# A gated linear-attention and mixer kernel: the recorded order of its 2,770 operations and their PSUM pools, exchanged from the conversion of w2 on

## The chip, the cores and the metric

The kernel runs on one core of one Trainium2 chip. The metric is the device time of one execution in microseconds (us), taken as the median of several runs. Beside the times there is one profiled execution, whose span (first to last instruction) is what every view of the trace shows.

## The reference

Two blocks follow each other. The first is a gated recurrence per head with a complex decay (4 batches, 8 heads, 768 steps, head dimension 48); the second a token mixer of rank 32 and a channel mixer (384 to 1536 to 384) on its output:

```
a_re_n, a_im_n = a_re * scale, a_im * scale        # scale = min(|a|, 0.999) / (|a| + 1e-6)
for t in range(S):
    S_re, S_im = ar*S_re - ai*S_im + k_t v_t^T, ar*S_im + ai*S_re
    y[:, :, t] = q_t @ S_re
x = y as (4, 768, 384)
u = x + (x^T @ U @ V)^T
out = u + relu(u @ w_ch1) @ w_ch2
```

All is float32.

## The kernel before, in words

**The work.** The 4 x 768 steps are cut into 24 chunks of 128 steps (six for each batch). Two neighbouring chunks form a group (12 of them), and two chunks also form one tile of the mixer (12 tiles, m = 0 to 11).

- For each group `gates` turns a_re and a_im into logarithms of magnitudes and into angles: ACT computes squares, logarithms, exponentials, arctangents and sines (L394), DVE adds and multiplies (L397, L400, L654, L673, L682, L683, L687, L771, L799, L801, L817), PE forms running sums of them (`es ps` and `ef ps` L699, `tot` L751, `ph` L806). Where a phase passes from one chunk to the next, POOL issues a small transfer that adds the last row of `F` onto the first row of the next chunk's angles (L788).
- `prep` multiplies q and k by the gates (L397, writing `qk` and `QKC`) and turns them over on PE (`tr` L873); ACT copies the result out (L884).
- `chain` does one chunk: masked products inside blocks (`inner` L923 and L920, `corners` L984), copied by DVE into `DG` (L935) and by four transfers on SP (L971) into `AT`; state updates `dk` (L1009), and the outputs `y` (L1040, L1048), which ACT copies to `xo`. All these products are small: `inner` L923 has 64 records on PE for 32 products of 32x48 columns.
- `mixer` does one mixer tile: `rank` L1083 and `mixed` L1102 mix tokens, `uTp` L1120 turns the result over, `up` L1135 (m = 0 to 2) or `few` L1235 (m = 3 to 11, with fewer products) goes to 1536 channels, `down` L1326 (m = 0) or L1369 comes back, DVE adds (L400) and the result leaves. For m = 0, `rT` L1149, `rw ps` L1158 and `fix` L1174 bring in the mixed tokens afterwards (DVE L1179).
- The weights come in as raw words in `stage` and are converted by ACT and DVE: for w2 two ACT operations (L394) and three on DVE (L587, L400, L589) for each of six pieces, then three differences of w2 (L617, written back into `stage`). Before m = 3, `combine` forms eight sums of w1 with 13 operations on DVE (L1288).

**The order.** Nothing of the order is left to the compiler. Each operation is handed to a `Plan` with an engine, a cost, the kind it belongs to, and what it reads and writes. `ORDER` holds, for each engine and kind, the place of every operation in one sequence from 0 to 2769; `Plan.order` sorts by these places, asserts that nothing comes before what it needs and that no buffer is taken before its last user, and the operations are issued in that sequence. Each engine and each queue (SP, POOL) takes its own in that order, and one that waits holds up all behind it on the same engine. `BANKS` gives each PSUM tile one of the pools T, A, Y and M (two buffers each). `SPARE` says after which places PE gets filler products of the identity (L1528), in units of 128 columns; a filler goes into a PSUM tile that is free and wide enough at that place.

```
for n in sorted(range(len(at)), key=lambda n: at[n]):
    assert not self.ops[n][5] - done, "an operation comes before what it needs"
...
    buffer(base, "ps" + BANKS[len(wide)], 2, shape, PSUM, padded)
```

The costs that the kernel's text still carries (`c_act`, `c_dve`, `c_dma`) play no part in the issue: the places are constants.

## Time and profile before

| what | us |
|---|---|
| median of 3 runs (lowest, highest) | 621.91 (621.03, 622.38) |
| profiled execution, own time | 619.11 |
| its span | 616.9 |
| PE busy | 598.9 |
| DVE busy | 531.5 |
| ACT busy | 401.8 |

The profiled execution's own time is 2.2 us over its span, and 2.8 us below the median of the runs. A busy PE is one that has a product in flight: products are pipelined, so a short wait between two of them does not show as idle time. PEld is the weight load that belongs to each product. In the views, a row names engine, line, output and input tiles; "issue" as the reason of an idle time means that the engine waited for nothing that the profile shows.

### The profile page before, as it was taken

Reading aid. Unit: us, or ns where it says so; the run is one execution under the profiler, and the core shown is the slowest. Engines: PE = TensorE matmul, PEld = TensorE weight load, DVE = VectorE, ACT = ScalarE, POOL = GpSimd, SP = SyncE. Lnnn points to the kernel's source line nnn. Section 1 sums busy time; section 2 is a strip of 40 time slices with the busy share of each in tenths; the row PEclk is TensorE's granted clock in tenths of the full one; section 3 lists DMA queues with packets and bytes.
Section 4 is the critical chain, followed back from the end, with each engine's and each line's share of the span. In section 5 each row is a group of like instructions: output and inputs, shape, how many; then the busy total and the mean of one; then the engine's idle time right before and its main releaser. Section 6 shows DMA issues by size and latency. Waiting matters only on the chain.

```text
span 616.9 us, 23966 instructions
## 1 busy us (share of the span) xinstructions
PE 598.9 (97%) x10572; PEld 526.8 (85%) x10572; DVE 531.5 (86%) x967; ACT 401.8 (65%) x789; POOL 36.3 (6%) x76
## 2 busy tenths in 40 slices
PE   6998989999999999999999999999999999999998
PEld 3566767656889979899999999899999998999997
DVE  6999999998999999999999999789889986464554
ACT  6999998989888896886696876565652622202020
POOL 4000000000000010000100100000110000000000
PEclk8999999999999999999999999999999999999999
DMA  9865565644233542521523331700122301000000
GB/s 214 198 148 114 136 133 140 157 126 92 50 57 80 92 85 48 109 54 32 113 49 59 86 70 34 137 9 3 39 54 52 65 9 20 21 7 7 20 20 26
DMA packets 173687, 45.77 MB, mean 74 GB/s; under 512 B 167632, under 2 KB 170384, under 8 KB 173584
## 3 DMA queue, kind: packets, MB, share of 16 engines
q1 hardware_dynamic: 171376, 39.90, 31.4%
q0 software_dynamic: 2208, 4.35, 2.1%
q8 instruction: 83, 1.36, 1.0%
q14 instruction: 20, 0.16, 0.1%
HBM read 33.59 MB, written 4.72 MB: 62 GB/s over the span
## 4 chain that ended last, share of the span: by engine, by line
PE 88%; ACT 8%; issue 1%; DVE 1%; DMA 1%; SPq 0%; ACTq 0%
PE down L1369 25%; PE few L1235 20%; PE up L1135 7%; PE dk L1009 4%; PE tr L873 4%; PE y L1048 3%; PE inner L923 3%; PE down L1326 2%; PE inner L920 2%; ACT gate L394 2%; PE y L1040 2%; PE tot L751 2%; PE mixed L1102 2%; PE rank L1083 1%; PE es ps L699 1%; PE up L1528 1%
## 5 line engine op out<-in xcount | busy, mean ns | idle before, releaser
L397 DVE TENSOR_TENSOR QK<-QK,T 96x512 f32<-96x512 f32 (+2 forms) x144 | 102.3, 725 | 1.5 <-PE corners L984 0.9
L1369 PE MATMUL down<-w,h 128*128 128x192 f32 x396 | 72.3, 330 | 0.0
L394 ACT ACTIVATE gate<-gate 128x768 f32<-128x768 f32 (+1 forms) x82 | 64.7, 795 | 9.3 <-DVE GS L801 5.5
L1369 PEld LDWEIGHTS down<-w,h 128*128 128x128 f32 x396 | 64.5, 190 | 1.3 <-issue 0.7
L884 ACT COPY QK<-tr 96x512 f32<-96x512 f32 x96 | 51.0, 587 | 16.9 <-PE tr L873 16.6
L1243 ACT COPY h<-few 128x512 f32<-128x512 f32 x54 | 31.1, 589 | 46.2 <-PE few L1235 34.3
L1135 PE MATMUL up<-uT,w 128*128 128x256 f32 x216 | 50.4, 385 | 0.0
L400 DVE TENSOR_TENSOR xo<-down,xo 128x192 f32<-128x192 f32 (+1 forms) x79 | 30.1, 384 | 23.1 <-PE down L1369 22.7
L1235 PE MATMUL few<-stage,w 128*128 128x128 f32 x360 | 47.1, 277 | 0.0
L1135 PEld LDWEIGHTS up<-uT,w 128*128 128x128 f32 x216 | 39.9, 190 | 5.5
L1235 PEld LDWEIGHTS few<-stage,w 128*128 128x128 f32 x360 | 44.0, 192 | 0.2
L1247 DVE CUSTOM_DVE_ANT_1 h<-few,h 128x512 f32<-128x512 f32 x54 | 35.9, 684 | 8.4 <-PE few L1235 7.0
L397 DVE TENSOR_TENSOR QKC<-qk,cs 128x768 f32<-128x768 f32 x44 | 41.7, 950 | 1.5 <-PE dk L1009 1.1
L989 ACT COPY AT<-corners 32x128 f32<-32x128 f32 x96 | 24.4, 257 | 24.6 <-PE corners L984 23.3
L1235 PE MATMUL few<-stage,sums 128*128 128x128 f32 x288 | 37.8, 278 | 0.0
L1369 PE MATMUL down<-stage 128*128 128x192 f32 x198 | 37.3, 330 | 0.0
L1235 PEld LDWEIGHTS few<-stage,sums 128*128 128x128 f32 x288 | 34.7, 192 | 0.6
L788 POOL DMA_DIRECT2D gate<-F x15 | 12.0, 799 | 362.6 <-DVE w L587 112.5
L1369 PEld LDWEIGHTS down<-stage 128*128 128x128 f32 x198 | 32.2, 190 | 1.0 <-issue 0.6
L873 PEld LDWEIGHTS tr<-ident,QKC 64*96 64x96 f32 x768 | 24.2, 123 | 10.0 <-issue 3.5
L400 DVE TENSOR_TENSOR h<-few,h 128x512 f32<-128x512 f32 x27 | 18.3, 686 | 16.4 <-PE few L1235 12.4
L873 PE MATMUL tr<-ident,QKC 64*96 64x64 f32 x768 | 29.4, 220 | 2.7 <-DVE QKC L397 1.6
(195 smaller groups left out, 1351.2 us busy)
## 6 DMA issues: line engine op xcount, KB each, us to landing
stage<-in_moe_w_ch_dram SPq DMA_DIRECT2D x12, 768.0 KB, 5.0
qk<-in_q_dram SPq DMA_DIRECT2D x24, 192.0 KB, 3.2
qk<-in_k_dram SPq DMA_DIRECT2D x24, 192.0 KB, 3.8
VP<-in_v_dram SPq DMA_DIRECT2D x24, 192.0 KB, 4.1
gate<-in_a_re_dram SPq DMA_DIRECT2D x22, 192.0 KB, 4.1
gate<-in_a_im_dram SPq DMA_DIRECT2D x22, 192.0 KB, 4.1
AT<-DG SPq DMA_DIRECT2D x96, 32.0 KB, 2.0
T<-E SPq DMA_DIRECT2D x48, 48.0 KB, 3.2
```

Of the source, the lines that this page charges most:

```text
L394: return nc.scalar.activation(out=o, in_=i, func=f, **kw)
L397: nc.vector.tensor_tensor(out=o, in0=a, in1=b, op=OP.mult)
L400: nc.vector.tensor_tensor(out=o, in0=a, in1=b, op=OP.add)
L873: nc.tensor.transpose(out=get(*ps[r])[0:DQ, h], in_=get(*qkc)[at, h * DQ:(h + 1) * DQ], identity=ident[at, at], tile_position=(r * HC, 0))
L884: nc.scalar.copy(out=to, in_=a)
L989: ACT(0.36, RR, lambda r=r, u=u: nc.scalar.copy(out=get(*ATi).rearrange("p (a u) t -> p a u t", u=2)[r:r + BLK, :, u, BLK:2 * BLK], in_=ge ...
L1009: nc.tensor.matmul(out=get(*dk[r])[x:x + w, h], lhsT=get(*ks)[at, h * DQ + x:h * DQ + x + w], rhs=get(*VPi)[at, h], start=True, stop=True, ...
L1135: nc.tensor.matmul(out=get(*ps)[:, e], lhsT=w1[:, f, (ff + e) * 128:(ff + e + 1) * 128], rhs=get(*uT)[:, f], start=(f == 0), stop=(f == KD ...
L1235: nc.tensor.matmul(out=get(*ps)[:, q], lhsT=w()[:, q * 128:(q + 1) * 128], rhs=v[0](), start=(n == 0 and q == 0), stop=True, skip_group_ch ...
L1243: ACT(c_act(n3 * CH) - 0.045, RU, lambda i=i, k=k: nc.scalar.copy(out=at(i, k), in_=get(*ps)), [ps], [o])
L1247: DVE(c_dve(n3 * CH), RU, lambda i=i, k=k: nc.vector._custom_dve(dve_ops.TENSOR_ADD_SAT, out=at(i, k), in0=get(*ps), in1=at(i, k), s0=math ...
L1369: nc.tensor.matmul(out=get(*to)[:, part], lhsT=x(j), rhs=y[:, j], start=(first and j == 0), stop=(j == KH - 1), skip_group_check=not first)
```

## The change

The change exchanges the three constants `BANKS`, `ORDER` and `SPARE`. No operation, cost, buffer or function is touched. The first 504 places are the same (up to about 100.5 us of the profiled execution); from there on nearly every place differs: that is the stretch in which the pieces of w2 are converted, m = 0 is finished, and everything behind it. In words it is said of the change that the search for the order charged transfers longer. By kind and engine the same operations are there; 18 units of filler stand behind place 504 before and after.

Cut to the lines on which the text below leans:

```diff
 BANKS = (
-    "...AAAAYYYTTTMMMMMMTTAAYYAATTMMTTTTMMMMMYMMAMAY"
+    "...AAAAYYYMTTAAAATYTYTTMMMMATAYTYATYMTYMMTYYTTATYTYMMYAYT"
...
 ORDER = {
-        ('ACT', 'w2'): {0: [513, 506], 2: [520, 535], 4: [608, 597], 6: [621, 627], 8: [655, 654], 10: [701, 702]},
-        ('DVE', 'w2'): {0: [534, 541, 542], 2: [586, 587, 588], 4: [616, 617, 619], 6: [640, 641, 646], 8: [661, 678, 682], 10: [711, 712, 713], 12:
-        [717, 725, 784]},
+        ('ACT', 'w2'): {0: [513, 507], 2: [575, 543], 4: [588, 602], 6: [630, 649], 8: [652, 655], 10: [707, 706]},
+        ('DVE', 'w2'): {0: [534, 561, 562], 2: [582, 594, 595], 4: [611, 612, 613], 6: [636, 658, 664], 8: [682, 683, 684], 10: [708, 709, 710], 12:
+        [763, 795, 837]},
...
-        ('POOL', 'angles'): {6: [614], 8: [706, 731], 10: [866, 912], 12: [1057], 14: [1265, 1312], 16: [1448, 1521], 18: [1698], 20: [1950, 2023],
+        ('POOL', 'angles'): {6: [616], 8: [700, 756], 10: [874, 934], 12: [1072], 14: [1267, 1292], 16: [1495, 1547], 18: [1731], 20: [1913, 1977],
...
-        ('DVE', 'mixing'): {3: [842, 845, 1024, 1078, 1098, 933, 1062, 1026, 1243, 1250, 1268, 1316, 1280]},
+        ('DVE', 'mixing'): {3: [637, 1027, 988, 1078, 1086, 659, 918, 754, 1098, 1103, 1221, 1247, 1288]},
 }
-SPARE = {20: 8, ... 436: 1, 595: 2, 600: 1, 605: 3, 623: 1, 631: 3, 645: 1, 652: 1, 663: 1, 693: 1, 694: 1, 715: 1, 716: 2}
+SPARE = {20: 8, ... 436: 1, 592: 3, 604: 2, 614: 1, 627: 3, 640: 1, 643: 1, 647: 1, 662: 1, 685: 1, 712: 1, 719: 1, 724: 2}
```

The small products keep their kinds but get other neighbours. Four places of the new sequence on PE, in the order of issue:

```
y L1040 x16, y L1048 x8 x8, inner L923 x32, dk L1009 ...        (chunks 7 and 8)
tr L873 x16, y L1040 x16, y L1048 x8 x8, dk L1009 ...           (chunks 9 and 10)
inner L920 x64, es ps L699, down L1369 ...                      (chunks 10 and 11)
y L1040 x16, y L1048 x8 x8, dk L1009, down L1369 ...            (chunks 13 and 14)
```

Three of the 13 operations of `combine` (places 842, 933 and 1026 before) come at 637, 659 and 754.

## The prediction

> **What bounds the kernel now.** First the page: busy times, the 40 slices, the queue of instruction transfers, and the chain that ended last (shares of it by engine).

> ```profile
> PE 598.9 (97%) x10572; PEld 526.8 (85%) x10572; DVE 531.5 (86%) x967; ACT 401.8 (65%) x789; POOL 36.3 (6%) x76
> ...
> PE   6998989999999999999999999999999999999998
> ...
> DVE  6999999998999999999999999789889986464554
> ...
> PEclk8999999999999999999999999999999999999999
> ...
> q8 instruction: 83, 1.36, 1.0%
> ...
> PE 88%; ACT 8%; issue 1%; DVE 1%; DMA 1%; SPq 0%; ACTq 0%
> ```

> PE carries 88% of the chain and is full from slice 7 on. DVE is full as well up to slice 25, so until about 380 us either can hold up the other; behind that DVE has room. The windows give the same by stage, from 100 us on, where the order begins to differ:

> ```profile
> 100.00:125.00 25.00, 24.91 (x480) 17.94 (x470) 23.34 (x38) 22.21 (x43) 0.96 (x1) 1.00 0.68 161
> 125.00:150.00 25.00, 24.57 (x132) 15.36 (x127) 22.42 (x31) 21.65 (x36) 0.77 (x1) 1.00 0.59 133
> 150.00:175.00 25.00, 24.58 (x403) 20.66 (x401) 23.40 (x37) 21.35 (x38) 1.36 (x2) 1.00 0.18 36
> ...
> 250.00:350.00 100.00, 100.00 (x1929) 93.69 (x1919) 97.15 (x183) 76.41 (x151) 7.99 (x12) 1.00 0.36 70
> 350.00:500.00 150.00, 149.32 (x3055) 141.19 (x3048) 134.32 (x255) 88.48 (x188) 9.34 (x15) 1.00 0.26 52
> ...
> 600.00:617.00 17.00, 13.91 (x86) 13.47 (x84) 7.72 (x18) 0.00 (x0) 0.00 (x0) 0.98 0.07 24
> ```

> The columns are PE, PEld, DVE, ACT and POOL busy, granted clock, DMA share and GB/s. The clock is full, and DMA is far from full behind 150 us. DVE is idle for 1.66, 2.58 and 1.60 us in the first three windows, and 2.85 us in the hundred from 250 on.

> Next, who waited for whom behind 100 us, on PE and (to 250 us) on DVE (us in total, times, longest):

> ```profile
> PE dk L1009 <- issue: 1.3, 2, 0.8
> PE inner L923 <- ACT F L394: 0.4, 1, 0.4
> PE tr L873 <- issue: 0.4, 1, 0.4
> PE down L1326 <- DVE h L1179: 0.3, 1, 0.3
> ...
> DVE xo L400 <- PE mixed L1102: 1.4, 2, 1.0
> DVE F L817 <- ACT F L394: 1.1, 2, 0.9
> DVE qk L397 <- DMA qk<-in_k_dram: 1.0, 1, 1.0
> ...
> DVE GS L799 <- DMA gate<-F: 0.2, 1, 0.2
> ```

> A wait of less than some 0.2 us is hidden on PE, because a product stays in flight that long. So I also added up start-to-start times, operation by operation, each at the median of its kind: from 100.9 us to its last product PE has 498.9 us of work of its own and takes 512.8. Some 5 of these 14 us are lost before 155 us, 2.6 in three holes (below), and the rest trickles, about 0.4 us in each 25 us. That is what another order can win from; nearly all of it before 160 us.

> **The change, part by part.**

> *The work itself: 0.* Counted in the listing of both kernels, every engine issues the same instructions, fillers apart, and these have the same sum (18 units of 128 columns). With the medians above, PE's own work comes to 498.8 us in the new order: turning from full to small products costs the same number of tenths. The last 16 us keep their order (`few`, then `down`, one addition, the last store), so the end behind the last product stays.

> *The holes that wait for "issue": +0.8 us.* All three lie in runs of small products:

> ```profile
> 219.04 0.58 PE L873 MATMUL tr<-ident,QKC 64*96 64x64 f32 x11
> 219.98 0.37 PE L873 MATMUL tr<-ident,QKC 64*96 64x64 f32 x5 [0.35 <-issue]
> ...
> 227.11 0.65 PE L873 MATMUL tr<-ident,QKC 64*96 64x64 f32 x16
> 227.69 0.68 PE L1040 MATMUL y<-VP,AT 64*64 64x48 f32 x32
> 228.31 0.67 PE L1048 MATMUL y<-GM,QK 96*64 96x48 f32 x16
> 228.81 0.64 PE L1048 MATMUL y<-G,QK 96*64 96x48 f32 x16
> 229.37 0.91 PE L1009 MATMUL dk<-VP,QKC 64*64 64x48 f32 x47
> 231.06 0.45 PE L1009 MATMUL dk<-VP,QKC 64*48 64x48 f32 x17 [0.78 <-issue]
> ...
> 358.62 0.56 PE L1009 MATMUL dk<-VP,QKC 64*48 64x48 f32 x26 [0.52 <-issue]
> ```

> The q8 row explains them: 83 transfers of 16.4 KB, against 2 x 10,572 products and weight loads and some 180 waits, make 256 instructions for each transfer. Counted that way, each hole begins exactly at a border between two blocks of 256 (127 records stand between 227.11 and the hole at 231.06). The three blocks in front of them last 2.4, 2.9 and 3.05 us without the hole and 3.1, 3.9 and 4.0 with it; no block of 3.5 us or more has a hole. So a block is there 3.1 to 4.0 us after the one ahead of it was begun, and a shorter one pays the difference.

> [...]

> In the new order I counted the same borders. Four blocks are shorter than 3.1 us: (chunk 7 and 8) `y` 29 and 32 records, `inner` L923 64; (9, 10) `tr`, `y` and `dk` as at 227 us; (10, 11) `inner` L920 117, `es ps`, `down`; (13, 14) `y`, `dk` 64. By the rows above and these

> ```profile
> 106.13 0.63 PE inner L920 x51
> ...
> 153.71 1.07 PE dk L1009 x57
> 154.79 0.82 PE inner L923 x64
> ...
> 600.17 13.75 PE down L1369 x84
> ```

> they last about 2.5, 2.95, 3.0 and 3.0 us. Against 3.7 us, the mean of the three, they pay 1.2 + 0.75 + 0.7 + 0.7 = 3.4 us, where the old order pays 0.65 + 1.0 + 0.95 = 2.6. At 3.1 us they would pay 0.9 (a gain of 1.7), at 4.0 us 4.5 (a loss of 1.9). I take +0.8.

> *Hand-offs between DVE and PE, 100 to 160 us: -0.4 us.* Two counts from durations of the trace, zero at the point where the orders part. Room: PE's own work up to an operation, less the work that stands on DVE up to the last result it needs. Lead: the work (PE, and what lies between) that must be done before a DVE operation has its input, less DVE's work before it. The worst of each, before / after, by PE's work since 100.9 us:

> | PE work, us | room | lead |
> |---|---|---|
> | 12 to 25 | -0.9 / 0.0 | 0.2 / 0.5 |
> | 25 to 37 | -0.3 / 0.4 | 0.9 / -0.1 |
> | 62 to 75 | 1.8 / -0.1 | 1.6 / -0.6 |
> | 100 to 112 | 2.1 / 1.1 | 2.4 / 1.1 |
> | 125 to 137 | 3.0 / 2.2 | 2.8 / 2.2 |
> | 200 to 212 | 4.3 / 4.4 | 3.9 / 4.0 |

> Room less lead is at worst -1.2 before and -0.5 after; from 100 us on the two are equally tight. That would be 0.7 us to win, at the place where PE loses its 5. But room falls by 1.9 at 62 to 75, for a reason that the trace prices: three sums of w1 are taken there early,

> ```profile
> L1288 DVE TENSOR_TENSOR sums<-w x4: 679/681/683, 178.3 to 259.6; 128x512 f32<-128x512 f32 x4
> ...
> L617 DVE TENSOR_TENSOR stage<-w,stage x2: 1351/1352/1352, 150.8 to 162.8; 128x1152 f32<-128x1152 f32 x2
> ```

> 3 x 0.68 = 2.0 us on DVE, in front of what PE needs. They cost nothing where DVE would be idle (5.8 us in the first three windows); without that cover they cost up to 1.9. The three L617, 4 us in all, come 7 to 16 us later, which relieves DVE at 148 to 151 us. Between a gain of 4 (most of the 5) and a loss of 1.9 I take what the two counts give, a little over half of 0.7.

> *Transfers: 0.* Only two waits for transfers on DVE behind 100 us are on record, 1.0 and 0.2 us (rows above), and one of 0.3 on ACT. The 1.0 is at 165.3: the k half of chunk 9, loaded after `QKC` of chunk 7 was done. In the new order that load stands behind four transfers of `DG` and the load of `VP` on SP and is used as soon; the wait may go or grow by about 1 us. The chain's transfer for `gate<-F` is better covered: between F (L817) and L799 DVE now has 3.6 us of other work (a product with `es`, a small copy and three of w2), against 2.5. Bounds -1.2 to +1, taken as 0. Behind every wait on SP stand the next loads; counted like room, the shortest time from landing to use changes by about 1 us either way (`AT` 3.6 us for 2.5, weights 4.5 for 5.3), and all of these stay covered.

> **Sum:** 0 + 0.8 - 0.4 + 0 = +0.4 us on 619.1, so 619.5 for an execution like the profiled one, and 621.9 + 0.4 = 622.3 us for the median of runs, which lies 2.8 us above it. A change within 0.2% (1.24 us) can't be told from none here, and this is one: no change that can be measured.

> **The rivals.**

> *Faster, 30%.* The 5 us that PE loses before 155 us are hand-offs, and the new order halves them: DVE has its inputs earlier everywhere up to 110 us (the lead column) and no operation of PE stands 0.9 us ahead of its input any more. For it: the idle rows `xo` <- `mixed` and `F` <- ACT, 2.5 us, are of this kind. Against it: DVE's own sum is not smaller. 2 to 4 us less with +0.8 of holes: 619.5 (618.3 to 620.5).

> *Slower by DVE's queue, 22%.* The early sums do not fall into idle time. Place: 125 to 175 us. Price 1.9 us and the 0.8 of the holes, 2.7: 624.6. It decides from the point where DVE is idle for less than 2 us between 125 and 165 us besides them; what stands behind them is the gates of group 5 and `prep` of chunks 6 and 7, for which PE has no other work in stock (room -0.1).

> *Slower by new waits that no count shows, 14%.* Tight everywhere to 380 us (DVE 97.15 of 100 us from 250 to 350), the new order meets four or five waits of 1 us, such as the load of 165 us, or all four starved blocks and those of 3.5 to 3.7 us: 3 to 6 us, 626.

> *The search does not do what it says:* longer charges cannot win where 1.2 us of waits for transfers are left on DVE. This is within the forecast.

> **How the numbers follow.** Forecast 34%, 621.1 to 623.5; faster 30%; slower 22 + 14%. The range leaves out a tenth at each side: below, a gain of 4 on the hand-offs and 0.7 on the holes, 617.6; above, the last rival with about 5 us, 627.0.

> **What would show it.** In the changed profile: PE behind 100 us has "issue" holes at four places instead of three, in `inner` or `dk` behind `y`, and none at `tr` behind L920; PE busy stays at 598 to 600; DVE's idle time in 100 to 175 us stays at 5 to 6.5 us; no wait for a transfer above 1.5 us. It is wrong if DVE idles less than 4 us there and PE reaches `down` L1369 earlier by 2 us or more (faster), if PE waits visibly for DVE between 125 and 175 us (slower), or if the blocks of 256 do not predict the holes.

## The result, and the profile after

The changed kernel takes 616.97 us (616.25 to 617.71, four runs) against 621.71 us (621.03 to 622.38) of the kernel before in the same measurement: a ratio of 0.9931, 95% interval 0.9914 to 0.9948. That is 4.7 us faster, below the range that was forecast (617.6 to 627.0 us). Measured again with more runs (below) it is 616.60 against 619.99 us, ratio 0.9943 (0.9927 to 0.9960), so 3.4 us; the four first runs of before lay high. Its profiled execution takes 616.25 us, with a span of 614.5 us.

The page of the kernel after, the same rows as were shown of before:

```profile
PE 597.1 (97%) x10572; PEld 526.5 (86%) x10572; DVE 531.4 (86%) x967; ACT 399.6 (65%) x789; POOL 36.9 (6%) x76
...
PE   6898989999999999999999999999999999999998
...
DVE  6999999999999999999999999889699986464653
...
PEclk9999999999999999999999999999999999999999
...
q8 instruction: 83, 1.36, 0.9%
...
PE 85%; ACT 7%; DVE 5%; DMA 1%; issue 1%; SPq 0%; DVEq 0%; ACTq 0%
```

Nothing here tells where 3 to 5 us went: the same work, the same 83 transfers of instructions. The windows (PE, PEld, DVE, ACT and POOL busy, clock, DMA share, GB/s) say a little more:

```profile
100.00:125.00 25.00, 24.56 (x476) 17.59 (x476) 23.07 (x38) 21.59 (x44) 0.96 (x1) 1.00 0.75 166
125.00:150.00 25.00, 24.74 (x166) 16.96 (x166) 24.34 (x36) 22.60 (x38) 0.77 (x1) 1.00 0.54 122
150.00:175.00 25.00, 24.52 (x579) 20.73 (x579) 24.23 (x37) 22.26 (x43) 1.36 (x2) 1.00 0.28 55
```

DVE idles 1.93 + 0.66 + 0.77 = 3.4 us from 100 to 175 us, where it idled 5.8: more work fits into this stretch. And all that PE still waits for visibly behind 100 us is this (us in total, times, longest), with the three waits for "issue" of before down to one:

```profile
PE y L1048 <- DVE QK L397: 0.4, 1, 0.4
PE rw ps L1158 <- DVE rw L1151: 0.4, 1, 0.4
PE down L1369 <- issue: 0.3, 1, 0.3
```

**A better ruler.** At some places of the two sequences PE has issued exactly the same products in both orders. The start of the next product there can be compared between any two profiles. Counted from such a product at 99.8 us in before, where the orders have not yet parted, the profiles of the runs below stand like this (us later than the first profile of before; negative is earlier):

| profile | at 109 | at 155.5 | at 213.7 | last product |
|---|---|---|---|---|
| before, first profile | 0 | 0 | 0 | 0 |
| before, second profile | 0.88 | 0.90 | 0.43 | 1.00 |
| after, first profile | -0.32 | -1.46 | -1.36 | -3.01 |
| after, second profile | -0.36 | -1.51 | -1.02 | -3.22 |

So about 1.5 us are won by 155 us, nothing from there to 214 us, and 1.7 to 2.2 us behind that. These are two different things, and the experiments take them apart.

**Pauses.** A "pause" below is the time from the start of the last record of a block of 256 instructions to the start of the next block's first record, where it is over 0.3 us, behind 100 us. (The idle time that a row shows is some 0.2 us less, as a product is in flight: in before 0.35, 0.78 and 0.52 us for the pauses of 0.57, 1.00 and 0.74; a record of `tr` or `dk` lasts 0.22 us.) Before has 0.57 + 1.00 + 0.74 = 2.3 us of them in its first profile and 2.9 in its second; after has 0.62 in its first, none in its second. Between long products the ordinary step is over 0.3 us too (0.32 between two of `down` L1326, 0.41 between two fillers), so some of the sums further down hold up to 0.7 us that is no wait.

### The profile page after: what moved, and what is told of

The parts are those of the page before. It is cut to its first block, busy times and chain, and to the rows that moved or that the text cites. A ratio compares the mean times of both kernels' runs of the same rounds, so it can differ in the third digit from the quotient of the medians.

```text
span 614.5 us, 23950 instructions
## 1 busy us (share of the span) xinstructions
PE 597.1 (97%) x10572; PEld 526.5 (86%) x10572; DVE 531.4 (86%) x967; ACT 399.6 (65%) x789; POOL 36.9 (6%) x76
## 3 DMA queue, kind: packets, MB, share of 16 engines
q8 instruction: 83, 1.36, 0.9%
## 4 chain that ended last, share of the span: by engine, by line
PE 85%; ACT 7%; DVE 5%; DMA 1%; issue 1%; SPq 0%; DVEq 0%; ACTq 0%
PE down L1369 25%; PE few L1235 20%; PE up L1135 7%; PE dk L1009 4%; PE tr L873 4%; PE y L1048 4%; PE inner L923 3%; PE inner L920 2%; PE y L1040 2%; ACT gate L394 2%; PE tot L751 2%; PE mixed L1102 1%; PE up L1528 1%; PE uTp L1120 1%; PE corners L984 1%
## 5 line engine op out<-in xcount | busy, mean ns | idle before, releaser
L397 DVE TENSOR_TENSOR QK<-QK,T 96x512 f32<-96x512 f32 (+2 forms) x144 | 101.1, 723 | 4.8 <-ACT QK L884 2.3
L1369 PE MATMUL down<-w,h 128*128 128x192 f32 x396 | 72.1, 330 | 0.0
L394 ACT ACTIVATE gate<-gate 128x768 f32<-128x768 f32 (+1 forms) x82 | 64.5, 796 | 4.9 <-DMA gate<-in_a_re_dram 1.8
L1369 PEld LDWEIGHTS down<-w,h 128*128 128x128 f32 x396 | 64.4, 190 | 1.3 <-issue 0.4
L400 DVE TENSOR_TENSOR xo<-down,xo 128x192 f32<-128x192 f32 (+1 forms) x79 | 29.8, 382 | 23.8 <-PE down L1369 23.5
L1135 PE MATMUL up<-uT,w 128*128 128x256 f32 x216 | 50.3, 385 | 0.0
L1135 PEld LDWEIGHTS up<-uT,w 128*128 128x128 f32 x216 | 40.0, 190 | 5.4
L397 DVE TENSOR_TENSOR QKC<-qk,cs 128x768 f32<-128x768 f32 x44 | 41.6, 950 | 1.7 <-ACT cs L394 1.1
L400 DVE TENSOR_TENSOR h<-few,h 128x512 f32<-128x512 f32 x27 | 18.3, 685 | 21.7 <-PE few L1235 13.2
L1369 PE MATMUL down<-stage 128*128 128x192 f32 x198 | 36.8, 330 | 0.0
L1369 PEld LDWEIGHTS down<-stage 128*128 128x128 f32 x198 | 32.3, 190 | 0.9 <-issue 0.6
L873 PEld LDWEIGHTS tr<-ident,QKC 64*96 64x96 f32 x768 | 24.0, 123 | 9.8 <-DVE QKC L397 3.3
L1311 POOL DMA_DIRECT2D out_dram<-xo x32 | 20.3, 677 | 190.3 <-DVE xo L400 112.4
```

The costliest lines, as they stand in the source:

```text
L394: return nc.scalar.activation(out=o, in_=i, func=f, **kw)
L397: nc.vector.tensor_tensor(out=o, in0=a, in1=b, op=OP.mult)
L400: nc.vector.tensor_tensor(out=o, in0=a, in1=b, op=OP.add)
L873: nc.tensor.transpose(out=get(*ps[r])[0:DQ, h], in_=get(*qkc)[at, h * DQ:(h + 1) * DQ], identity=ident[at, at], tile_position=(r * HC, 0))
L1135: nc.tensor.matmul(out=get(*ps)[:, e], lhsT=w1[:, f, (ff + e) * 128:(ff + e + 1) * 128], rhs=get(*uT)[:, f], start=(f == 0), stop=(f == KD ...
L1369: nc.tensor.matmul(out=get(*to)[:, part], lhsT=x(j), rhs=y[:, j], start=(first and j == 0), stop=(j == KH - 1), skip_group_check=not first)
```

## The experiments

### Repeats, and half of each order

First both kernels again, with many runs.

> The kernel before, unchanged, run again: how far two profiled executions of one order differ, and how far its times scatter. Both theories (hand-offs between 100 and 200 us; pauses at the borders of the instruction blocks) expect a ratio of 1.000 within 0.2%. The block theory expects pauses on PE at the same five borders as in the first profile (59.7, 95.8, 220, 231 and 358.6 us, 0.6 to 1.5 us each), since the instruction count decides them; if they were chance, they would stand elsewhere.

Measured: 620.50 us against 620.11, ratio 1.0000 (0.9990 to 1.0009). The pauses at 221, 232 and 360 us and the one at 96 us came again at the same products; the one at 59.7 did not. It also shows a stall that the first profile has not, of 0.72 us of idle time, to which we return.

> The changed kernel, unchanged, against the kernel before on one chip with many runs. The two profiles differ by 3.0 us from 100 us on (2.4 us in the span), the medians of the first four runs each by 4.7 us. If the profiles are typical: 617.1 against 620.1 us, a ratio of 0.995. If the first medians are: 0.9925. PE reaches the product behind place 740 (155 us) about 1.5 us earlier than before counted from 101 us, and the blocks of instructions pause PE only near 307 us after 100 us.

Measured: 616.60 against 619.99 us, ratio 0.9943 (0.9927 to 0.9960): between the two forecasts, nearer to the profiles. PE reached 155 us 1.5 us earlier, as expected, and there was no pause over 0.3 us behind 100 us at all.

Then sequences made of both: the first 950 places of one, the rest in the sequence of the other; each PSUM tile keeps the pool that it has in the half where it begins (but for two tiles behind the seam in the first of the two runs).

```diff
-        ('POOL', 'angles'): {6: [614], 8: [706, 731], 10: [866, 912], 12: [1057], 14: [1265, 1312], ...
+        ('POOL', 'angles'): {6: [616], 8: [700, 756], 10: [874, 934], 12: [1058], 14: [1265, 1312], ...
```

> The order of after up to place 950 (about 196 us), then the remaining operations in the order of before. At the cut the same products stand behind both on PE, so every later block of 256 instructions begins at the same product as in before. Hand-off theory: what after gains up to 196 us (1.9 us between the two profiles, by PE's start of place 950 less the 0.56 us of the common part) stays to the end: 619.8 us against 621.7, PE 1.9 us early from 200 us on, DVE idle 100 to 175 us near 3.4 us. Block theory: the pauses at 220, 231 and 358.6 us are there as in before, and the time is that of before, 621.7.

Measured: 619.29 us, ratio 0.9988 (0.9979 to 0.9998). In its profile 1.49 us are won at 155 us; the seam at place 950 then costs 0.8 us (`down` waits for an addition of DVE), and 1.45 are left at the end. The pauses at 219 and 230 us are there (0.83 and 1.01), that at 357 is not. The early gain is real and comes with the first half of the order, though the times show 0.8 us of the 1.9 that the hand-off theory said.

With the halves exchanged:

> The order of before up to place 950 (about 197 us), then the remaining operations in the order of after. Hand-off theory of the stretch 100 to 200 us: nothing is won up to 197 us, and what is left is at most 1.0 us, so 620.7 to 621.7. Block theory: the pauses at 220, 231 and 358.6 us (2.3 us in all) go and one of 0.6 at 307 us comes, as in after: 1.7 us faster, 620.0. If the early half gives 1.9 and this half 1.7 or less, both have a part.

Measured: 621.49 us, ratio 1.0011 (0.9999 to 1.0023), slower than either theory said. The seam again: two products of PE start 2.3 us apart at 198.8 us, and its profile ran with a granted clock of 0.5 for 3.4 us twice, from 97.1 us and, right behind the seam, from 202.9 us. PE stands 0.4 us early at 196 us and 3.7 us late at 214. Behind 214 us, past the seam, it wins 2.2 us and has no pause. So the late gain belongs to the late half, but the time alone would not have shown it.

### The early part: pools of PSUM

The prediction had asked only when an operation has its data. A PSUM tile also needs a buffer, and `BANKS` gives it one of two in its pool. In before 19 of the 31 tiles that begin between 116 and 155 us take pool T, among them all running sums (`ef ps`, `es ps`, `tot`). On PE:

```profile
135.73 1.30 PE L699 MATMUL ef ps<-GS,fore 128*128 128x384 f32 x4
136.97 0.62 PE L699 MATMUL es ps<-GS,mid 128*128 128x384 f32 x2
137.61 0.86 PE L751 MATMUL tot<-total,GL 128*96 128x32 f32 x8
138.55 0.62 PE L699 MATMUL es ps<-GS,mid 128*128 128x384 f32 x2
```

The same products in after:

```profile
135.71 0.92 PE L699 MATMUL ef ps<-GS,fore 128*128 128x384 f32 x2
136.46 0.52 PE L699 MATMUL es ps<-GS,mid 128*128 128x384 f32 x2
136.81 0.52 PE L699 MATMUL ef ps<-GS,fore 128*128 128x384 f32 x2
137.17 0.52 PE L699 MATMUL es ps<-GS,mid 128*128 128x384 f32 x2
137.52 1.47 PE L751 MATMUL tot<-total,GL 128*96 128x32 f32 x16
```

From 136.46 on the running sums follow each other every 0.35 us in after, and `tot` comes 1.8 us behind the first; in before the last `es ps` starts only at 138.55. Their data was there at 135.9 in before and at 136.1 in after. But in before four of these tiles start 0.05 us after DVE or ACT has emptied the buffer that they need (`ef ps` of chunk 8 is emptied at 136.91, `es ps` starts at 136.97). No idle time of PE shows, since each wait is no longer than a product stays in flight (0.2 to 0.3 us in the rows of PEld below; a record of `es ps` L699 lasts 0.34 us in the median); it shows in the starts. And it shows in the rows of PEld, the weight load, from 134 to 140 us, which the prediction did not use: in before (two rows for "issue" left out)

```profile
PEld tot L751 <- ACT gate L394: 0.3, 1, 0.3
...
PEld ef ps L699 <- DVE F L817: 0.3, 1, 0.3
PEld es ps L699 <- ACT gate L394: 0.3, 1, 0.3
PEld es ps L699 <- ACT es L394: 0.2, 1, 0.2
```

1.1 us in four waits, each for the reader of the tile that had the buffer before; in after one row is left, and it waits for data:

```profile
PEld ef ps L699 <- DVE GS L683: 0.3, 1, 0.3
```

In after the buffers of the four running sums have been free for 5 to 15 us.

To test it, the order of before got other pools for 27 of the 31 tiles:

```diff
 BANKS = (
-    "...MMMMMMTTAAYYAATTMMTTTTMMMMMYMMAMAY"
-    "YYTTMYMMTTTTTTTTTTTTTTTTTTAAATYYM..."
+    "...MMMMMMAYYMTAYYMAATMMYMMMMMMYMMAMAY"
+    "YYTTMYMMTTTTTTTMTMMAMMMTMYYYATYYM..."
```

> The order of before, every place kept; only the PSUM pools of the 27 tiles that begin between places 590 and 740 (116 to 155 us) differ: each takes the pool whose older buffer has been free the longest, where before nearly all of them share the pool T. Theory of the pools: the hand-offs at which PE begins 0.05 us after ACT or DVE has emptied the older buffer of T (ef ps, es ps and tot of chunks 8 and 9 at 136.4, 137.0, 137.6 and 138.6 us, mixed at 119.1, tr at 150.8) lose that wait: 1.2 to 1.8 us less by 155 us, and as much at the end, 618.5 to 619. Theory of the order (who stands behind whom on DVE and ACT): no change, 620.1. Block theory: no change, since no product is added or moved.

Measured: 619.99 us, ratio 1.0001 (0.9982 to 1.0020): no gain. The waits at 136 to 139 us did go, but the new pools made another:

```profile
155.28 1.13 PE L1009 MATMUL dk<-VP,QKC 64*64 64x48 f32 x60 [1.19 <-DVE uT L1126]
```

Half of `dk` had got the buffer of a `uTp` that DVE empties late. A pool chosen by the order of issue is not one chosen by time. So the trial was repeated with five tiles, chosen by the times in the trace:

```diff
 BANKS = (
-    "...MMMMMMTTAAYYAATTMMTTTTMMMMMYMMAMAY"
-    "YYTTMYMMTTTTTTTTTTTTTTTTTTAAATYYM..."
+    "...MMMMMMTTAAYYAATAMMTTTTMMMMMYMMAMAY"
+    "YYTTMYMMTTTTTTTTTTYYYTTTTYAAATYYM..."
```

> The order of before, every place kept; only five PSUM tiles change their pool: mixed 1 of m = 0 (T to A), ef ps and es ps of chunk 9, tot of chunk 8 and one tr of chunk 6 (T to Y). By the trace of before none of the tiles between 116 and 151 us then begins less than 0.5 us after its buffer was emptied, and none of them waits for a buffer that is emptied late, as dk did in the trial with 27 tiles (1.4 us at 153.9). Theory of the pools: 1.0 to 1.6 us less than before at 155 us and at the end, 618.4 to 619 against 620.0. Theories of transfers and of blocks: no change, 620.0; the pauses at 220, 231 and 359 us stay.

Measured: 619.01 against 620.03 us, ratio 0.9985 (0.9973 to 0.9996). From 109 to 155 us its profile wins 1.0 us, and holds it to 214 us. And the other way round:

```diff
 BANKS = (
-    "...MMMMATAYTYATYMTYMMTYYTTATYTYMMYAYT"
-    "YMTTYAMMMMTTATMTAAYTTATMAYTY..."
+    "...MMMMATTTTYATYMTYMMTYYTTATYTYMMYAYT"
+    "YMTTYAMMMMTTATTTTTTTTTTMAYTY..."
```

> The order of after, every place kept; seven PSUM tiles between places 592 and 677 (ph and rT and rw ps of m = 0, ef ps, es ps twice and tot of chunks 8 and 9) are put back into the pool T. Theory of the pools: the serial hand-offs between PE and ACT at 136 to 139 us come back, 1.0 to 1.8 us more than the kernel after, 618 to 619 against 617. Theory of the order: no change against after.

Measured: 619.70 us, ratio to before 0.9995 (0.9970 to 1.0021), 3.1 us over after in the medians, with a wide scatter (616.6 to 623.7). In the profile it is 0.16 us late at 155 us where after is 1.46 early: 1.6 us, and most of it lies here:

```profile
135.32 1.00 PE L699 MATMUL ef ps<-GS,fore 128*128 128x384 f32 x2
136.15 0.51 PE L699 MATMUL es ps<-GS,mid 128*128 128x384 f32 x2
137.27 0.62 PE L699 MATMUL ef ps<-GS,fore 128*128 128x384 f32 x2 [0.61 <-ACT gate L394]
138.03 0.62 PE L699 MATMUL es ps<-GS,mid 128*128 128x384 f32 x2
```

The pools are worth 1.0 to 1.6 us in this stretch, whichever order they are tried in. That the medians set this kernel 3.1 us over after goes with the granted clock: six of its runs, its profile among them, have a mean granted clock of 1.0 and take 616.6 to 619.0 us (median 618.0), the other six have 0.989 to 0.994 and take 620.4 to 623.7. The three runs of after at 1.0 take 615.9 to 616.5, so 1.9 us less.

### The early part: one small transfer

The stall of the second profile of before, and the same place in after:

```profile
105.64 0.59 PE L699 MATMUL ef ps<-GS,fore 128*128 128x384 f32 x2
106.96 0.79 PE L1040 MATMUL y<-VP,AT 64*64 64x48 f32 x32 [0.72 <-issue]
```

```profile
105.48 0.59 PE L699 MATMUL ef ps<-GS,fore 128*128 128x384 f32 x2
105.91 0.51 PE L699 MATMUL es ps<-GS,mid 128*128 128x384 f32 x2
106.25 0.51 PE L699 MATMUL ef ps<-GS,fore 128*128 128x384 f32 x2
106.60 0.51 PE L699 MATMUL es ps<-GS,mid 128*128 128x384 f32 x2
107.04 0.69 PE L920 MATMUL inner<-QK 96*16 96x16 f32 x64
107.67 0.75 PE L1040 MATMUL y<-VP,AT 64*64 64x48 f32 x32
```

"issue" is here a transfer: `y` of chunk 4 reads `AT`, and the last of the four transfers of 32 KB (L971) landed at 106.87 in this run, 5.5 us after its issue, where the median of all 96 is 2.0 us; `q`, `k`, `VP`, `gate` and w2 are loaded at the same time (DMA share 1.05 from 100 to 105 us). `y` starts 0.09 us behind it. For the transfers of L971 in this run the trace gives

```profile
DMA to landing us min/median/max: 1.9/2.0/5.5
```

In the first profile of before it landed 4.8 us after its issue and `y` followed 0.39 us later, without a stall. In after three running sums and `inner` stand ahead of `y`, which starts 1.5 us behind the landing. To test it, the order of after was kept to place 590 only:

```diff
-        ('ACT', 'w2'): {0: [513, 506], 2: [520, 535], 4: [608, 597], 6: [621, 627], 8: [655, 654], 10: [701, 702]},
+        ('ACT', 'w2'): {0: [513, 507], 2: [575, 543], 4: [588, 599], 6: [621, 627], 8: [655, 654], 10: [701, 702]},
```

> The order of after up to place 590 (101 to 116 us), then the order of before; on PE the two have then issued the same products. In that stretch after puts the running sums es ps and ef ps of chunks 6 and 7 ahead of y of chunk 4, whose last small transfer into AT lands 4.8 to 5.5 us after its issue. Theory of the transfers: y of chunk 4 begins over 1 us behind that transfer, where before has 0.1 to 0.4 us, and the stall of 0.9 to 1.0 us near 106 us that two of the repeats of before's order show is gone in every execution: 0.3 to 1.3 us less, 618.7 to 619.7. Theory of the pools: no change behind 116 us, so 620.0 if the transfers cost nothing. Block theory: no change.

Measured: 620.76 us, ratio 1.0008 (0.9991 to 1.0024), so no gain. At 109 us it is 0.36 us early, as every profile with this start is (-0.29 to -0.36 in eleven of them, against -0.02 to +0.88 in nine with the start of before). But behind the seam `rT` L1149 starts 0.9 us after the product ahead of it, because ACT converts a piece of w2 (0.97 us) and makes an `h` before it empties `rank` for it; at 155 us this kernel is 0.60 late.

This start and the five pools together:

> Both edits at once: the order of after up to place 590, then the order of before, with the five tiles in other pools. If transfers and pools are two separate causes, the gains add: 1.5 to 2.8 us less than before, 617.2 to 618.5, and PE reaches the product behind place 740 (155 us) 1.4 to 1.6 us earlier than in the first profile of before, counted from 100 us, as after does. What is then left to after (616.6) is the pauses at the borders of blocks, 1.2 to 1.7 us.

Measured: 619.49 us, ratio 0.9991 (0.9978 to 1.0003). At 155 us 0.34 us are won, not 1.5: the start's 0.34 stay, the seam eats what the pools give. That the two gains add is not shown by it.

### The late part: where the blocks of 256 begin

To move the borders and nothing else, early groups of fillers were issued in pieces: the same columns in more products, within the first 36 us, where PE still has idle time (in before it is busy for 18.7 of the first 25 us). Each product more is four records (8 of them make 16 more on PE and 16 on PEld, 10,588 for 10,572 each), and all later borders fall that much earlier in the sequence.

```diff
-            idle(min(run, AHEAD))
-            run -= min(run, AHEAD)
+            k = min(run, 1 if at in (20, 82) else AHEAD)
+            idle(k); run -= k
```

That is the shift by 32 records; (20, 32, 119) makes 64, (20, 32, 82, 119, 140) makes 96, and with 113 and 153 added it is 128.

> The order of before, but two early groups of filler products are issued in pieces of 128 columns: 8 products (32 records of PE and its weight loads) more with the same columns, all before 15 us, so that every later border of a block of 256 lies 32 records earlier in the order. Nothing else differs. Block theory: the pauses at 59.7, 95.8, 220, 231 and 358.6 us (4.5 us in all) go or shrink, one of up to 0.6 us may come near 307 us: 2 to 4 us faster, 617.7 to 619.7. Hand-off theory: no change, 621.7, since no operation has another neighbour.

Measured: 621.87 us, ratio 1.0027 (1.0017 to 1.0037): slower, where the block theory had promised 2 to 4 us. But the pauses still stand at the borders, and these now lie between other products. For example:

```profile
218.78 0.66 PE L920 MATMUL inner<-QK 96*16 96x16 f32 x60
220.50 0.22 PE L920 MATMUL inner<-QK 96*16 96x16 f32 x4 [1.05 <-issue]
...
309.09 1.02 PE L1009 MATMUL dk<-VP,QKC 64*64 64x48 f32 x54
311.05 0.38 PE L1009 MATMUL dk<-VP,QKC 64*48 64x48 f32 x10 [0.94 <-issue]
```

The first one cuts `inner` after 60 of its 64 records, where the border in before cut `tr`, 32 records later in the sequence. Four pauses and one ordinary step of `down` (0.32) make 4.9 us. The mechanism held; the size was wrong, because new borders bring new pauses.

A shift of only 8 records (the condition is `at == 157`), on top of the start and the five pools:

> As the run with both edits, and one early group of fillers is issued in pieces of 128 columns: two products (8 records) more with the same columns, so that every later border of a block of 256 lies 8 records earlier in the order. Block theory: the border at 231 us then no longer falls beside the waits of tr, and that at 359 us falls among long products, so both pauses (1.0 and 0.7 us) go, the one at 220 us stays at 0.9 us, and one of 0.1 us may come near 308 us: 1.2 to 1.6 us less than the run with both edits, 615.8 to 617.2, the time of after. Theories of pools and transfers: no change against the run with both edits.

Measured: 621.11 us, ratio 1.0017 (1.0005 to 1.0029), a miss of the same kind: the pauses at 232 and 360 us stayed (1.28 and 0.92) and two came.

The kernel after, shifted by 96:

> The order and the pools of after; five early groups of fillers are issued in pieces of 128 columns, 24 products (96 records) more with the same columns, before 35 us, so that every later border of a block of 256 lies 96 records earlier in the order. Block theory: where after has one pause behind 100 us (0.6 us), this one gets five to seven of 0.3 to 0.9 us, by the lengths of its blocks near 110, 174, 220, 271, 457 and 487 us (each under 3 us): 2 to 3.5 us slower than after, 619 to 620.5. Theories of pools and order: as after, 617.

Measured: 622.77 us, ratio to before 1.0047 (1.0030 to 1.0064): 6.2 us slower than after, by 24 small products in the first 33 us. Two of its five pauses:

```profile
110.19 0.38 PE L984 MATMUL corners<-QK 96*32 96x32 f32 x20
111.85 0.32 PE L984 MATMUL corners<-QK 96*32 96x32 f32 x12 [1.27 <-issue]
```

```profile
177.08 0.66 PE L1009 MATMUL dk<-VP,QKC 64*64 64x48 f32 x28
179.17 0.78 PE L1009 MATMUL dk<-VP,QKC 64*64 64x48 f32 x36 [1.43 <-issue]
```

Pauses: 1.47 + 1.64 + 0.86 + 0.81 + 0.89 = 5.7 us. What was open then was whether any of the late gain is the order's own, so the same shifts were given to both. (The runs of the shifts come from three chips, on which before took 620.0 to 620.4 us.)

> The order and pools of before; 16 early products (64 records) more with the same columns, so that later borders of blocks lie 64 records earlier in the order. Block theory: by the lengths of the blocks in the trace of before, pauses of 1.2 us near 219, 0.6 near 305, 0.4 near 456 and 1.1 near 487 us in place of those at 220, 231 and 359 us: 3.2 us in all in place of 2.3, so 621 against 620.0. Theory that only the order counts: 620.0.

> The same 64 records more in the kernel after. Block theory: pauses of about 0.9 us near 109, 173, 456 and 487 us and 0.4 near 316 us, 4.1 us in all where after has 0.6 to 1.1: 3 us slower than after, 619.6, and only 1.4 us faster than before with the same shift. Theory that the gain belongs to the order wherever the borders fall: 616.6 or 3.4 us less than before with the same shift.

> The order and pools of before with 32 early products (128 records) more. Block theory: pauses of 1.5 us near 194, 1.1 near 219, 0.2 near 329 and 0.4 near 407 us, 3.3 us in all: 621 to 621.4. Theory that only the order counts: 620.0.

> The same 128 records more in the kernel after. Block theory: pauses of 1.2 us near 173, 0.8 near 191, 1.0 near 218 and 0.3 near 329 us, 3.5 us in all: 2.4 us slower than after, 619.0, and 2 us faster than before with the same shift, which is what pools and transfers give. Theory that the gain belongs to the order alone: 616.6.

> The order and pools of before with 24 early products (96 records) more, the shift that cost after 6 us. Block theory: pauses near 195, 219, 456 and 487 us, 3 to 4 us in all against 2.3 in before: 620.5 to 622, below the 622.8 of after with the same shift, whose pauses came to 5.7 us. Theory that only the order counts: 620.0, and after 3.5 us below it.

> The order and pools of after with 8 early products (32 records) more, the shift with which before took 621.9. Block theory: pauses near 109, 173, 305 and 456 us, 2 to 3 us in all. The three shifts of after measured so far lie on one line, 615.8 us and 1.23 us for each us of pauses (0.6: 616.6; 3.4: 619.8; 4.6: 621.3; 5.7: 622.8), so 618.3 to 619.5. Theory that only the order counts: 616.6.

Ratios to before, in this order: 0.9988 (0.9972 to 1.0004), 0.9995 (0.9977 to 1.0013), 1.0027 (1.0008 to 1.0045), 1.0017 (0.9999 to 1.0035), 1.0016 (1.0002 to 1.0031), 1.0031 (1.0014 to 1.0048). All shifts together (time, and the sum of the pauses in the profile):

| shift, records | before: us | pauses | after: us | pauses |
|---|---|---|---|---|
| 0 | 620.0 to 620.5 | 2.3 and 2.9 | 616.60 | 0.6 and 0 |
| 32 | 621.87 | 4.9 | 622.27 | 4.9 |
| 64 | 619.43 | 3.4 | 619.83 | 3.4 |
| 96 | 621.09 | 3.0 | 622.77 | 5.7 |
| 128 | 621.53 | 3.7 | 621.34 | 4.6 |
| mean | 620.8 | 3.5 | 620.6 | 3.8 |

The block theory was right in the sign for after at each shift (3.2, 4.7 and 5.7 us slower at 64, 128 and 32, expected 3, 2.4 and 1.7 to 2.9) and near the time for before at 96 and 128; for before it was wrong at 32 and at 64, which became a little faster. For after the five points (0.3 us of pauses at shift 0) lie on a line, 616.1 us and 1.17 us for each us of pauses, within 0.45 us; for before the slope is 0.7, with up to 1.3 us beside it. Averaged over the five shifts the two orders are as good as equal in these medians, as if the new order had no gain of its own.

The profiles say more. Each run lists its mean granted clock, and in the profiles of after shifted by 96 and by 32 the clock is halved for 3.4 us beside one of the long pauses (the one of 1.47 us, which ends at 111.85, and the one of 2.0, which ends at 177.52; the one of 1.64 at 179 us in the first of them has none):

```profile
113.70:117.10 3.40, 3.40 (x10) 2.68 (x9) 3.02 (x5) 1.99 (x4) 0.00 (x0) 0.50 0.88 259
```

```profile
177.30:180.70 3.40, 3.17 (x11) 2.55 (x12) 3.19 (x6) 0.84 (x2) 0.78 (x1) 0.50 0.21 34
```

On the ruler PE loses 3.3 us there for the pause of 1.47, and 3.7 for the one of 2.0: about 1.8 us each beside the pause. In these two kernels 9 and 7 of 12 runs have a mean granted clock under 0.996, in before 49 of 161. Whether a long pause brings the low clock is not shown, but the low clock is part of the 1.17. With the runs at 0.996 or more alone (3 to 11 for each shifted kernel, 6 of after), the medians for the shifts 0, 32, 64, 96 and 128 are 619.9, 621.6, 619.4, 620.9 and 620.5 us for before and 616.0, 620.5, 619.3, 621.9 and 621.6 for after: after is 0.6 us faster in the mean. And the ruler at the last product, less the sum of the pauses, gives -2.3 us for before and -3.3 for after in the mean of the five shifts, so 1.0 us for the order itself; without the two halved clocks it would be 1.7 (an estimate: 2 x 1.8 us over five shifts). That is the size of the early gain.

So the distance between the two kernels as they stand has two parts: some 1.5 us that the order and its pools win before 155 us, and 1.7 to 2.9 us of pauses that after misses, because its borders fall where they cost nothing. The second part is not the order's own: each of the four shifts took it away.

No version tried beats the changed kernel.

## Why the prediction was wrong, point by point

**What bounds the kernel; the work itself, 0.** Right. PE is the bound, its work is the same (597.1 for 598.9 us busy), the end behind the last product too.

**The holes that wait for "issue", +0.8: this step failed.** It found the mechanism and even the blocks: the four that it named last 2.50, 2.91, 2.9 and 3.0 us (forecast 2.5, 2.95, 3.0, 3.0) and end at 191, 229, 246 and 308 us. But only the last of them paid over 0.2 us (0.62 and 0.23 in two profiles). In place of 3.4 us after pays 0 to 0.6, where before pays 2.3 to 2.9 (2.6 was taken): a gain of 1.7 to 2.9, not a loss of 0.8 (the gain at the lower bound of the rule, 3.1 us, was 1.7). The rule "a block is there 3.1 to 4.0 us after the one ahead of it was begun" was taken from three holes behind 100 us. Ahead of 100 us the same trace has two that contradict it (the waits of PE from 50 to 100 us):

```profile
PE inner L920 <- issue: 1.3, 1, 1.3
...
PE dk L1009 <- issue: 0.5, 1, 0.5
```

They are the pauses at 95.8 and 59.7 us, at borders too, and the blocks in front of them last 4.4 and 5.1 us without the pause. The transfer of the next block does not begin at a fixed time after PE has entered a block. Before the three pauses of before behind 100 us it began 0.82, 1.32 and 1.63 us after PE had crossed the border into the block that proved too short, and before the two earlier ones 3.54 and 3.37 us after it; at the three blocks of after without a pause it began 0.82, 0.65 and 0.71 us before PE crossed it, as if the stream of instructions were read ahead of PE by a varying stretch. Most of these transfers take 0.9 to 1.5 us, and at all 71 pauses over 0.45 us behind 50 us, in all the profiles, the next block starts 1.2 to 1.7 us after the end of its transfer; so a block of 2.5 us is enough in the one case and one of 3.3 us is too short in the other. This is read from the starts of the transfers in the traces. What sets the lead is only argued: at the three blocks of after some long products (`down` L1369, `up` L1135) stand within 60 records ahead of the border, at those of before waits for semaphores stand beside it, but one border of after has both. The forecasts for the shifted kernels went by the lengths of the blocks; they placed some of the pauses and missed others.

**Hand-offs between DVE and PE, -0.4: mis-sized, for a reason.** At 155 us after is 1.5 us early. Room and lead counted when data is ready and left out the PSUM buffers, though their pools were named in the change. 1.0 to 1.6 us of it are the pools (shown in both orders). The early sums L1288 cost nothing that shows: DVE's idle time took them in, it fell by 2.4 us there, and PE's waits did not grow. The gain lies below what PE's waits list, since each (0.2 to 0.3 us in PEld's rows) was no longer than a product is in flight (0.34 us for `es ps`); those rows had 1.1 us of it.

**Transfers, 0: failed by 0.3 to 1.2 us.** It looked at the loads of DVE's inputs and at the shortest time from landing to use in one profile. The use that matters, `y` of chunk 4 behind `AT` at 105 us, had 0.39 us in that profile and 0.09 in four others with the same start. Here the change does what is said of it: a transfer is given more time.

**The sum.** By the two profiles of after: -1.5 at 155 us, +0.1 to +0.5 to 214 us, -1.7 to -2.2 behind it, -3.0 to -3.2 in all; the times say -3.4 (11 runs against 34) and -4.7 (four each). The first profiled execution of before was 2.8 us quicker than the median beside it; the second, 1.0 us later at the last product through the stall and larger pauses, shows where a part of that comes from. Why the first four runs set the two kernels 1.3 us further apart is not explained.

**The rivals.** "Faster" named the right place for the early part but the wrong cause (DVE's inputs), and carried the +0.8 of the holes with it, so that its best case, 618.3, was still too slow. The two slower ones did not happen. The sign set down for being wrong, DVE idle under 4 us from 100 to 175 us, came (3.4); "PE earlier by 2 us or more" came only behind 229 us.

**Open.** What sets how far ahead of PE the transfer of a block begins. Whether a pause of 1.5 us or more brings the half clock beside it. And how much of the early gain lasts over all shifts: the medians of all runs give 0.2 us, those at a granted clock of 0.996 or more 0.6, the profiles 1.0 to 1.7.

## What to carry to other kernels

Read starts, not only idle time: a chain of products that each start 0.05 us behind the emptying of their PSUM buffer cost about a third of a microsecond each here and appeared in no row of PE, only in those of its weight loads (0.2 to 0.3 us each), so look there, and lay out for each tile when its buffer was emptied, beside when its data was ready. In a program of many small products, see whether pauses for "issue" stand at multiples of 256 instructions; if they do, a comparison of two orders is worth little until both have been run with their borders shifted, because a shift alone moved one order by 6 us and the other by 2.4. Compare the granted clock of the runs as well: in one kernel here it split the times into two groups 3.7 us apart. And one profile of a stretch with loads in flight may be the lucky one: of two profiles of before the first has no stall at 106 us, the second one of 0.72 us.
